# Moving 344 KB of the second dense matrix to the lower half of the partitions, and its products to the early sum

## Chip, cores, metric

One core of one Trainium2 chip. The metric is the device time of one execution in microseconds (us). The kernel before took 192.01 us (median of 4 runs, 191.77 to 192.2).

## What is computed

One decode step for two sequences: a layer norm of `x`, then attention over a window of 4096 cached positions, and beside it a dense layer with the mish activation; the two results and `x` are summed.

```python
xn = _layernorm(x, axis=-1)
return x + _A_ref(xn, k_cache, v_cache, wq, wo) + _B_ref(xn, w1, b1, w2)

# B: D = 448, F = 1792, two rows
h = einsum("bsd,df->bsf", x, w1) + b1
act = h * tanh(softplus(h))
out = einsum("bsf,fd->bsd", act, w2)
```

`w2` is 1792 rows of 448 bf16 numbers, 1.6 MB. The keys, the values and the four weight matrices together are 77.7 MB, and every byte of them is used once.

## The kernel before

**Stages.** The 8 key/value heads and 2 sequences are taken in U = 4 units (`u`), each with four pairs of sequence and head. A unit's keys are two tiles of 4 MB (`load_k`, two halves), its values four tiles of 2 MB (`load_v`, `g` = 0 to 3). Per unit, the vector engine transposes the keys (`turns`, line 267), TensorE makes the scores (`scores`, line 345), ScalarE the exponentials (line 353), and TensorE weighs the values (`values`, line 390). `gather`, `finish` collect the unit's output; `relay` and `mix_early` multiply it by its rows of `wo`.

**Two sums in PSUM.** `early` is a [2, 448] sum of full width: one matmul adds 448 columns. It takes `x` and the units 0 to 2 (`mix_early`, line 472). `carry` copies it to SBUF and from there into `acc`, a sum that is cut into four column groups of 112; `add_rows` (line 247) adds to `acc` with four matmuls, one for each group. The last unit (`mix`) and all of the second dense matrix (`dense_out`) go to `acc`. At the end `acc` is copied to `res` and stored.

**The dense layer.** `w1` is loaded early and used in unit 0 (`dense_in`), then `mish` makes `act_bf`, [128 partitions, 7, 2, 2]. The 1792 inner rows are cut in two halves `k` of 896; partition `p` holds rows 7p to 7p+6 of each half, so `act_bf[p, i, k]` meets row `7p + i` of half `k`. `w2` is loaded in four parts at the very end of the stream, into a buffer of the pool that held the keys: all 7 rows of half 0, then rows 0 to 3, 4 and 5, and 6 of half 1 (`w2_parts`, line 536).

**Order of the transfers.** All large transfers are issued by the SyncE queue (SP) in the order of the program: for each unit u = 0 to 2 the first keys of the next unit, two value tiles, the second keys, two value tiles, the unit's rows of `wo`; then for u = 3 two value tiles, `wo` in two transfers, the third value tile, the fourth in two pieces (24 and 8 of 32 columns), and the four parts of `w2`. An issue waits where its buffer isn't free yet (two buffers for keys and `w2`, three for values) and where its completion semaphore is still held: eight such semaphores are used in turn, so a transfer can't be issued until the eighth transfer before it has landed. `x` and the bias `b1` are issued by ScalarE's queue.

**The last unit on TensorE**, in order: `values(3, 0)`, then `relay(2)`, `mix_early(2)` and `carry()`, then `values(3, 1)`, `values(3, 2)`, `gather`, the fourth value tile (`values_fixed`, line 425), `finish`, `mix`, `dense_out` of the four parts, and the copies to `res`.

Of the kernel before, what the change touches and what calls it, by code (L numbers as in the profile page):

```python
# [11 lines left out]
BF16 = mybir.dt.bfloat16  # L12
FP32 = mybir.dt.float32
# [4 lines left out]
def kernel(  # L18
# [13 lines left out]
    nc = tc.nc  # L32
    P = 128
# [3 lines left out]
    RK = 2  # L37

    Bsz, Sq, D = A_x.shape
# [20 lines left out]
    NI = F2 // P  # L60
# [7 lines left out]
    k_pool = ctx.enter_context(tc.tile_pool(name="kk", bufs=2))  # L68
# [4 lines left out]
    consts = ctx.enter_context(tc.tile_pool(name="consts", bufs=1))  # L73
# [7 lines left out]
    ps_m = ctx.enter_context(tc.tile_pool(name="ps_m", bufs=1, space=PSUM))  # L81

    KE = T * Dh
# [3 lines left out]
    def ring(name):  # L87
        return v_pool.tile([P, KE], BF16, tag="v", name=name)
# [9 lines left out]
    def load_v(u, g, lo=0, hi=T):  # L98
        if lo == 0:
            v_t[u, g] = ring("v")  # L100
        t = v_t[u, g]
        src = vview[u][:, s0:, :].rearrange("j (g x t) d -> g x j (t d)", g=G, x=C)
        nc.sync.dma_start(  # L103
            out=t[:, lo * Dh : hi * Dh], in_=src[g, :, :, lo * Dh : hi * Dh]
        )
# [16 lines left out]
    x_bf = consts.tile([Bsz, D], BF16)  # L122
    nc.scalar.dma_start(out=x_bf[:, :], in_=A_x.flatten_outer_dims())
    b1_sb = consts.tile([P, 2, NI], BF16)
    nc.scalar.dma_start(out=b1_sb[:], in_=B_b1.rearrange("(k q c) -> q k c", k=2, q=P))

    load_k(0, 0)
    wq_t = []
# [7 lines left out]
    ident = consts.tile([P, P], BF16)  # L136
# [9 lines left out]
    for k in range(KU):  # L146
        nc.gpsimd.tensor_copy(
            out=hot[:, k, :, :, k], in_=ident[:].rearrange("p (q y) -> p y q", y=4)
        )
    eps_t = consts.tile([Bsz, 1], FP32)  # L150
    nc.vector.memset(eps_t[:], 1e-5)

# [6 lines left out]
        out=rstd[:], in_=mv[:, 1:2], func=ACT.Sqrt, bias=eps_t[:], scale=1.0  # L159
# [4 lines left out]
        out=xn_bf[:],  # L164
# [8 lines left out]
        out=parm[:], in_=ident[:].rearrange("p (a o) -> p o a", o=2), axis=AXIS.X, op=ALU.add  # L173
# [3 lines left out]
        out=jm[:],  # L177
        in_=ident[:].rearrange("p (a j h) -> p j a h", j=J, h=rep),
# [4 lines left out]
        out=jm[:], in0=jm[:], scalar1=-1.0, scalar2=29952.0, op0=ALU.add, op1=ALU.mult  # L183
# [3 lines left out]
        out=mneg[:], in_=jm[:].unsqueeze(1).to_broadcast([P, TH * 8, J])  # L187
    )
    sel = consts.tile([P, 2, NQ], FP32)
    for x in range(2):  # L190
        for w in range(4):
            at = 32 * w + (2 * (w % 2) + x) * NQ
# [3 lines left out]
            else:  # L196
                nc.vector.tensor_tensor(
                    out=sel[:, x, :], in0=sel[:, x, :], in1=src, op=ALU.add
# [16 lines left out]
    for odd in range(2):  # L215
        for half in range(2):
            o = (half + odd) % 2
            nc.vector.tensor_scalar(
                out=xs[:, odd::2, half * Bsz : (half + 1) * Bsz],
# [6 lines left out]
    early = ps_e.tile([Bsz, D], FP32)  # L226
# [5 lines left out]
    def carry():  # L232
        e_sb = small.tile([P, 2 * Dh], FP32, tag="vs", name="e_sb", bufs=1)[0:Bsz, 0:D]
        nc.scalar.copy(out=e_sb, in_=early[:])
        for g in range(G):
            nc.tensor.matmul(
                acc[32 * g : 32 * g + Bsz, :],
                lhsT=id2[:],
                rhs=e_sb[:, g * DG : (g + 1) * DG],
                start=True,  # L240
                stop=False,
                skip_group_check=True,
            )
# [31 lines left out]
    for n in range(2):  # L275
        for e in range(2):
# [3 lines left out]
                out=sp[:],  # L280
                in_=ident[:, o : o + 63 : 2].unsqueeze(1).to_broadcast([P, G, 32]),
# [81 lines left out]
    state = {}  # L363
# [18 lines left out]
    def values(u, g):  # L382
        if g == 0:
            state["v", u] = ps_v.tile([P, 2, Dh], FP32, tag="v", name="pv")
        pv = state["v", u]
        v = v_t.pop((u, g))
        for k in range(T // 2):
            a, b = k // 2, k % 2
            w = 2 * (a % 2) + b
            nc.tensor.matmul(  # L390
                pv[32 * w : 32 * (w + 1), :, :].rearrange("p x d -> p (x d)"),
                lhsT=p_t[a // 4][:, g, 4 * (a % 4) : 4 * (a % 4) + 4, :].rearrange(
                    "p t q -> p (t q)"
                ),
                rhs=v[:, 2 * k * Dh : (2 * k + 2) * Dh],
                start=(g == 0 and a < 2),
                stop=(g == G - 1 and a >= 6),
                skip_group_check=True,
            )
# [46 lines left out]
    def relay(u):  # L446
        oT = state.pop(("oT", u))
        ox_ps = ps_m.tile([P, 4, 2, Bsz], FP32, tag="m", name="ox_ps")
        for h in range(rep):
            rows = slice(h * 64, (h + 1) * 64)  # L450
            for y in range(4):
                for k in range(KU):
                    nc.tensor.matmul(
                        ox_ps[rows, y, :, :],
                        lhsT=hot[:, k, y, :, :].rearrange("p q k -> p (q k)"),
                        rhs=oT[:, :, k * rep + h, :],
                        start=(y == 0 and k == 0),
                        stop=(y == 3 and k == KU - 1),
                        skip_group_check=True,
                    )  # L460
        ox = small.tile([P, 8, Bsz], BF16, tag="ox", name="ox")
        nc.scalar.copy(  # L462
            out=ox[:].rearrange("p i b -> p (i b)"),
            in_=ox_ps[:].rearrange("p y c b -> p (y c b)"),
        )
        state["ox", u] = ox

    def mix_early(u):
        ox = state.pop(("ox", u))
        w = wo_t.pop(u)[:].rearrange("p k h (c d) -> p (k h c) d", c=2)  # L470
        for i in range(8):
            nc.tensor.matmul(  # L472
                early[:],
                lhsT=ox[:, i, :],
                rhs=w[:, i, :],
                start=False,
                stop=(u == U - 2 and i == 7),
            )
# [8 lines left out]
    act_bf = consts.tile([P, NI, 2, Bsz], BF16)  # L487
# [24 lines left out]
    def mish():  # L512
        h_ps = state.pop("h")
        shape = [P, NI, 2, Bsz]
        h_sb = consts.tile(shape, FP32, name="h_sb")
        nc.vector.tensor_tensor(
            out=h_sb[:],
            in0=h_ps[:],
            in1=b1_sb[:].rearrange("p k i -> p i k").unsqueeze(3).to_broadcast(shape),
            op=ALU.add,  # L520
        )
        u_sb = consts.tile(shape, FP32, name="u_sb")
        nc.scalar.activation(out=u_sb[:], in_=h_sb[:], func=ACT.Exp)
        t_sb = consts.tile(shape, FP32, name="t_sb")
        nc.vector.scalar_tensor_tensor(
            out=t_sb[:], in0=u_sb[:], scalar=2.0, in1=u_sb[:], op0=ALU.add, op1=ALU.mult
        )
        den = consts.tile(shape, FP32, name="den_sb")
        nc.vector.tensor_scalar(
            out=den[:], in0=t_sb[:], scalar1=2.0, scalar2=None, op0=ALU.add  # L530
        )
        nc.vector.reciprocal(out=den[:], in_=den[:])
        nc.vector.tensor_tensor(out=t_sb[:], in0=t_sb[:], in1=den[:], op=ALU.mult)
        nc.vector.tensor_tensor(out=act_bf[:], in0=h_sb[:], in1=t_sb[:], op=ALU.mult)

    w2_parts = ((0, 0, NI), (1, 0, 4), (1, 4, 6), (1, 6, NI))

    def load_w2(part):
        if part == 0:
            state["w2"] = k_pool.tile([P, RK * KE], BF16, tag="k", name="w2")  # L540
        k, lo, hi = w2_parts[part]
        w2_in = B_w2.flatten().rearrange("(k p e) -> k p e", k=2, p=P)
        at = k * NI * D
        nc.sync.dma_start(  # L544
            out=state["w2"][:, at + lo * D : at + hi * D],
            in_=w2_in[k, :, lo * D : hi * D],
        )
# [13 lines left out]
    turns(0, 1)  # L561
    dense_in()
    mish()
    scores(0, 1)
    weigh(0)
    for u in range(U - 1):
# [18 lines left out]
        if u < U - 2:  # L585
            relay(u)
            mix_early(u)
    u = U - 1
    load_v(u, 0)
    load_v(u, 1)  # L590
    load_wo(u)
# [3 lines left out]
    for part in range(len(w2_parts)):  # L595
        load_w2(part)
    for g in range(G - 1):
        values(u, g)
        if g == 0:
            relay(u - 1)  # L600
            mix_early(u - 1)
            carry()
# [48 lines left out]
```

## Time and profile before

| | |
|---|---|
| median of 4 runs | 192.01 us |
| the profiled execution, its own time | 191.54 us |
| its span, first to last instruction | 189.4 us |
| first data packet of the stream | about 2.2 us after the start |
| last landing of an input | 186.44 us |
| moved by DMA | 77.78 MB, 411 GB/s over the span |
| VectorE busy | 89.4 us (47%) |
| TensorE matmuls busy | 85.5 us (45%) |
| ScalarE busy | 12.3 us (7%) |

All times below are counted from the start of the span. A transfer is said to land when the last of its sixteen completion marks (the semaphore events of the trace, one for each DMA engine) has come.

### The profile page before, as it was taken

To read this page: it belongs to the slowest core of one execution; us is meant where nothing else is said; L and a number is where in the kernel's file an instruction comes from. 1 tells how busy PE (TensorE), PEld (TensorE's weight loads), DVE (VectorE), ACT (ScalarE), POOL (GpSimd) and SP (SyncE) were. 2 spreads that over 40 slices of the span, in tenths; PEclk is the share of its full clock that TensorE was granted. 3 is DMA by queue.
4 is the path that set the end of the run, shared out by engine and by line. 5 is a ranking of instruction groups with operands and counts; after the bars stand their busy time and mean duration, and the time that the engine had idled before them with its cause. 6 is when DMAs were issued, how large, how long until landed. Compare 5 with 4: busy or idle time off the path is not lost.

```text
span 189.4 us, 1986 instructions
## 1 busy us (share of the span) xinstructions
PE 85.5 (45%) x870; PEld 37.0 (20%) x873; DVE 89.4 (47%) x81; ACT 12.3 (7%) x23; POOL 3.9 (2%) x16
## 2 busy tenths in 40 slices
PE   0301645455039004878335023867256044956484
PEld 0100121421012001423012011412011011522183
DVE  6619642983990098018940395038910692040001
ACT  3000031001000000110001000110001001011001
POOL 8000000000000000000000000000000000000000
PEclk9999999999999955566858855586756655599555
DMA  6999999999999999999999999999999999999990
GB/s 222 443 384 418 458 422 418 454 439 394 429 491 415 384 420 434 434 436 429 415 460 443 398 412 478 407 415 419 436 450 412 415 424 434 432 398 429 407 382 31
DMA packets 5871, 77.78 MB, mean 411 GB/s; under 512 B 868, under 2 KB 1640, under 8 KB 2408
## 3 DMA queue, kind: packets, MB, share of 16 engines
q1 hardware_dynamic: 5588, 77.66, 96.8%
q8 instruction: 6, 0.10, 0.2%
q10 hardware_dynamic: 276, 0.01, 0.1%
q14 instruction: 1, 0.01, 0.0%
HBM read 77.67 MB, written 0.00 MB: 410 GB/s over the span
## 4 chain that ended last, share of the span: by engine, by line
DMA 82%; PE 8%; DVE 3%; issue 3%; SPq 2%; ACT 1%; DVEq 0%
DMA v<-in_A_v_cache_dram 59%; DMA k<-in_A_k_cache_dram 15%; DMA w<-in_B_w_dram 7%; PE pv L390 4%; DVE kt L267 2%; PE sc L345 2%; PE o L410 1%; DVE p L356 1%; SPq L132 1%; SPq L544 1%; SPq L95 1%; SPq L103 0%; ACT ex L353 0%; PE acc L247 0%; ACT vs L404 0%
## 5 line engine op out<-in xcount | busy, mean ns | idle before, releaser
L267 DVE STREAM_TRANSPOSE kt<-k 128x4096 f32<-128x4096 f32 x16 | 70.1, 4420 | 41.4 <-DMA k<-in_A_k_cache_dram 41.4
L390 PE MATMUL pv<-v,p 128*32 128x512 bf16 x240 | 25.1, 562 | 61.4 <-DMA v<-in_A_v_cache_dram 61.4
L345 PE MATMUL sc<-kt,qd 128*32 128x512 bf16 x256 | 24.8, 554 | 4.6 <-DVE kt L267 2.3
L390 PEld LDWEIGHTS <-p 128*32 128x32 bf16 x240 | 8.2, 120 | 77.2 <-issue 69.3
L437 DVE TENSOR_TENSOR oT<-o,rec 128x16 bf16<-128x16 f32 x4 | 0.7, 174 | 30.9 <-PE o L410 16.6
L356 DVE STREAM_TRANSPOSE p<-ex 128x512 bf16<-128x512 bf16 x8 | 5.2, 690 | 14.6 <-ACT ex L353 14.6
L345 PEld LDWEIGHTS <-qd 128*32 128x32 bf16 x256 | 8.1, 126 | 18.3 <-issue 15.5
L353 ACT ACTIVATE ex<-sc 128x512 bf16<-128x512 f32 x8 | 4.8, 597 | 73.9 <-PE sc L345 73.9
L289 PE MATMUL q_ps<-wq,xs 128*32 128x512 bf16 x28 | 3.4, 625 | 12.1 <-DMA wq<-in_A_wq_dram 12.1
L410 PE MATMUL o<-sel,vs 128*128 128x8 f32 x32 | 7.5, 364 | 2.8 <-ACT vs L404 2.8
L410 PEld LDWEIGHTS o<-sel,vs 128*128 128x128 f32 x32 | 7.1, 326 | 6.4 <-ACT vs L404 6.4
L472 PE MATMUL early<-wo,ox 128*2 128x448 bf16 x24 | 8.0, 499 | 0.8 <-ACT ox L462 0.8
L368 PE MATMUL dn<-p,ones 128*128 128x512 bf16 x8 | 3.5, 434 | 6.4 <-DVE p L356 6.4
L404 ACT COPY vs<-pv 128x512 f32<-128x512 f32 x4 | 2.3, 585 | 54.0 <-PE pv L390 54.0
L502 PE MATMUL h_ps<-xs,w 128*128 128x4 bf16 x49 | 2.8, 193 | 4.3 <-DMA w<-in_B_w_dram 4.3
L210 PE MATMUL xr_ps<-ident,xrows 2*128 2x2 bf16 x7 | 1.0, 181 | 6.6 <-DVE xrows L209 6.6
L376 DVE TENSOR_REDUCE rec<-dn 128x8 f32<-128x512 f32 x4 | 2.8, 692 | 2.1 <-PE dn L368 2.1
L289 PEld LDWEIGHTS <-xs 128*32 128x32 bf16 x28 | 1.0, 126 | 14.0 <-issue 14.0
L502 PEld LDWEIGHTS <-w 128*128 128x128 bf16 x49 | 2.7, 154 | 5.2 <-DMA w<-in_B_w_dram 5.2
L472 PEld LDWEIGHTS <-ox 128*2 128x2 bf16 x24 | 2.3, 105 | 4.6 <-issue 3.0
L334 PE MATMUL sc<-mneg,ident 128*128 128x512 bf16 x5 | 3.0, 591 | 0.0
L368 PEld LDWEIGHTS <-ones 128*128 128x128 bf16 x8 | 0.5, 99 | 8.2 <-DVE p L356 5.9
(62 smaller groups left out, 38.0 us busy)
## 6 DMA issues: line engine op xcount, KB each, us to landing
k<-in_A_k_cache_dram SPq DMA_DIRECT2D x8, 4096.0 KB, 30.3
v<-in_A_v_cache_dram SPq DMA_DIRECT2D x15, 2048.0 KB, 27.3
wo<-in_A_wo_dram SPq DMA_DIRECT2D x3, 896.0 KB, 24.8
wq<-in_A_wq_dram SPq DMA_DIRECT2D x1, 2048.0 KB, 16.9
w<-in_B_w_dram SPq DMA_DIRECT2D x1, 1568.0 KB, 32.2
wq<-in_A_wq_dram SPq DMA_DIRECT2D x1, 1536.0 KB, 19.9
v<-in_A_v_cache_dram SPq DMA_DIRECT2D x1, 1536.0 KB, 11.6
wo<-in_A_wo_dram SPq DMA_DIRECT2D x2, 448.0 KB, 15.5
```

The lines of the kernel that those rows point to most:

```text
L267: nc.vector.transpose(out=kt[i][:, :, :, r, :], in_=t[:, r * KE : (r + 1) * KE].bitcast(FP32).rearrange("p (a c j) -> p a c j", c=P // (R ...
L289: nc.tensor.matmul(q_ps[32 * u : 32 * (u + 1), :], lhsT=xs[:, s, :], rhs=wq_t[s][:, u * 512 : (u + 1) * 512], start=(s == 0), stop=(s == N ...
L334: nc.tensor.matmul(sc[:].rearrange("p t c m -> p (t c m)"), lhsT=ident[:], rhs=mneg[:].rearrange("p a j -> p (a j)"), start=True, stop=Fal ...
L345: nc.tensor.matmul(sc[32 * w : 32 * (w + 1)].rearrange("p t c m -> p t (c m)"), lhsT=qd[:, u, 2 * n + e, :, :].rearrange("p g q -> p (g q) ...
L353: nc.scalar.activation(out=ex[:, :, :, i, :], in_=sc[:], func=ACT.Exp, scale=scale)
L356: nc.vector.transpose(out=p_t[h][:].rearrange("p g t q -> p t g q"), in_=ex[:, h * TH : (h + 1) * TH].rearrange("p t c i m -> p t (c i m)" ...
L368: nc.tensor.matmul(dn[:].rearrange("p a q -> p (a q)"), lhsT=ones[:], rhs=p_t[i][:].rearrange("p g t q -> p (g t q)"), start=(i == 0), sto ...
L376: nc.vector.tensor_reduce(out=rec[:], in_=dn[:].rearrange("p a q -> p q a"), axis=AXIS.X, op=ALU.add)
L390: nc.tensor.matmul(pv[32 * w : 32 * (w + 1), :, :].rearrange("p x d -> p (x d)"), lhsT=p_t[a // 4][:, g, 4 * (a % 4) : 4 * (a % 4) + 4, :] ...
L410: nc.tensor.matmul(po[:, c, :], lhsT=sb[:, x, c::2], rhs=sel[:, x, :], start=(x == 0 and c == 0), stop=(last and x == 1), skip_group_check ...
L472: nc.tensor.matmul(early[:], lhsT=ox[:, i, :], rhs=w[:, i, :], start=False, stop=(u == U - 2 and i == 7),)
L502: nc.tensor.matmul(h_ps[:, i, :, :].rearrange("p k b -> p (k b)"), lhsT=w1_v[:, s, i, :], rhs=xs[:, s, 0 : 2 * Bsz], start=(s == 0), stop= ...
```

## The change

Rows 0 to 2 of the 7 rows that a partition holds of half 1 (128 x 3 x 896 B = 344 KB) no longer come with the other parts of `w2` at the end. They are loaded before the values of the last unit, onto partitions 0 to 63 only: partition 32z + 4a + b takes those of old partition 64h + 32z + 8b + a, for h = 0 and h = 1 one behind the other. Four transfers of 32 partitions with 2688 B each carry them; by the name of the change DMA engines 0 to 7 do. `act_low` holds the activations in the same new order: `mish` makes it with two matmuls against columns of the identity (`perm`) and a copy. Six matmuls of full width (`dense_out_low`, over 64 partitions) add the products to `early`, after `values(3, 0)`. The remaining parts of `w2` are three, and the load of `b1` is cut in five transfers.

```diff
-    nc.scalar.dma_start(out=b1_sb[:], in_=B_b1.rearrange("(k q c) -> q k c", k=2, q=P))
+    b1_in = B_b1.rearrange("(k q c) -> q k c", k=2, q=P)
+    for lo, hi in ((0, 64), (64, 80), (80, 96), (96, 112), (112, P)):
+        nc.scalar.dma_start(out=b1_sb[lo:hi], in_=b1_in[lo:hi])
...
+    perm = consts.tile([P, 4, 8, 4], BF16)
+    nc.gpsimd.tensor_copy(
+        out=perm[:], in_=ident[:].rearrange("p (z b a) -> p z a b", b=4, a=8)
+    )
...
+        ap_ps = ps_m.tile([P, 2, LOW, Bsz], FP32, tag="m", name="ap_ps")
+        for h in range(2):
+            nc.tensor.matmul(
+                ap_ps[0 : P // 2, h, :, :],
+                lhsT=perm[:, 2 * h : 2 * h + 2].rearrange("p z a b -> p (z a b)"),
+                rhs=act_bf[:, 0:LOW, 1, :],
+                start=(h == 0),
+                stop=(h == 1),
+                skip_group_check=True,
+            )
+        nc.vector.tensor_copy(out=act_low[:], in_=ap_ps[0 : P // 2])
-    w2_parts = ((0, 0, NI), (1, 0, 4), (1, 4, 6), (1, 6, NI))
+    LOW = 3
+    act_low = consts.tile([P // 2, 2, LOW, Bsz], BF16)
+    w2_parts = ((0, 0, NI), (1, LOW, 6), (1, 6, NI))
+    low_at = 2 * NI * D
+
+    def load_w2_low():
+        state["w2"] = k_pool.tile([P, RK * KE], BF16, tag="k", name="w2")
+        w2_in = B_w2.flatten().rearrange("(k h z b a e) -> k h z a b e", k=2, h=2, z=2, a=8, b=4)
+        for h in range(2):
+            at = low_at + h * LOW * D
+            for z in range(2):
+                nc.sync.dma_start(
+                    out=state["w2"][32 * z : 32 * (z + 1), at : at + LOW * D],
+                    in_=w2_in[1, h, z, :, :, 0 : LOW * D],
+                )
+
+    def dense_out_low():
+        for h in range(2):
+            for i in range(LOW):
+                at = low_at + (h * LOW + i) * D
+                nc.tensor.matmul(
+                    early[:],
+                    lhsT=act_low[:, h, i, :],
+                    rhs=state["w2"][0 : P // 2, at : at + D],
+                    start=False,
+                    stop=False,
+                )
...
     u = U - 1
+    load_w2_low()
     load_v(u, 0)
...
         if g == 0:
+            dense_out_low()
             relay(u - 1)
             mix_early(u - 1)
             carry()
```

## The prediction

> **What bounds the kernel now.** I read the page's slices first, then the chain of waits, the DMA queues, and the completion marks in the trace.
>
> ```profile
> span 189.4 us, 1986 instructions
> ...
> DMA  6999999999999999999999999999999999999990
> ...
> q1 hardware_dynamic: 5588, 77.66, 96.8%
> q8 instruction: 6, 0.10, 0.2%
> ...
> q14 instruction: 1, 0.01, 0.0%
> ```
>
> The DMA row is the reading: from the second slice to the last but one the sixteen engines have no free time. Nothing on TensorE or VectorE can shorten the run unless the last bytes land earlier. The two lines "instruction" are fetches of program code that use the same engines; inside the span there are six of 16 KB and one of 8 KB. The end of the chain of waits:
>
> ```profile
> 172.06 0.05 issue
> 172.12 14.07 DMA w<-in_B_w_dram
> 186.19 0.04 issue
> 186.23 0.60 PE acc L247 x12
> 186.83 0.24 DVE res L617
> ```
>
> The chain hangs on the last two parts of `w2` (landed 186.19 and 186.44); 12 matmuls, the copies and the store follow. So the question is when the slowest of the sixteen engines ends. The sixteen marks of three transfers, sorted, from the trace's semaphore events:
>
> ```
> w1 (3.25)      35.01 35.03 35.05 35.09 35.11 35.17 35.19 35.22 35.23 35.24 35.25 35.27 35.31 35.33 35.44 35.49
> k, unit 1      64.25 64.26 64.27 64.33 64.34 64.39 64.41 64.43 64.46 64.46 64.47 64.54 64.57 64.70 66.04 66.20
> w2, last part  184.40 184.51 184.52 184.59 184.61 184.61 184.64 184.69 184.73 184.83 185.55 186.06 186.18 186.22 186.38 186.44
> ```
>
> At 35 us all engines are within 0.48 us. After two code fetches (39.84 and 62.80) two are some 1.5 us late. At the end six are late: five by about 1.5 us and one by 0.75 us, ten are not. The packet that shares its engine with a 16 KB fetch shows why: the fetch takes 0.97 to 1.11 us, and the next packet 0.47 to 0.50 us longer than its neighbours (1.71 for 1.21). The lateness is never made up, since no engine is ever idle. The sixth large fetch (183.95) moved no mark; it fell on an engine that had ended.
>
> **What the change does to the marks.** Every engine carries the same bytes before. A part of 3584 B a partition (8 packets an engine) sets the marks 1.06 us later, one of 1792 B 0.56, one of 896 B some 0.25 to 0.30. Between them 8 packets of 2688 B cost 0.81.
> - Taken from every engine at the end: 1.06 + 0.56 - 0.81 = 0.81 us (six rows of half 1 become three).
> - Added to engines 0 to 7: four transfers of 32 x 2688 B on eight engines are 16 packets an engine, 2 x 0.81 plus three marks of 9 ns = 1.65 us.
> - So engines 8 to 15 end 0.81 us earlier, and engines 0 to 7 0.84 us later.
>
> The trace doesn't number the engines. If the six late ones are all in 8 to 15, the late ones end at 186.44 - 0.81 = 185.63 and the latest of the others at 184.83 + 0.84 = 185.67: 0.77 us earlier than now. If a late one is in 0 to 7, it ends at 186.06 to 186.44 + 0.84 = 186.90 to 187.28. These are the two bounds, -0.77 and +0.84, and between them I take the first by the nearest rows: the first packets of the stream start between 2.176 and 2.437, and in that order, followed packet by packet up to each fetch, the engines hit first, third and fifth (39.84, 96.95, 164.95) are tenth, fourteenth and fifteenth of sixteen. If the engines start in the order of their numbers, these three are in 8 to 15. But the one hit by the 8 KB fetch is eighth, and those hit second and fourth belong to a cluster of three that I can't tell apart (second, sixth and twelfth), so that order can hold only in part. The evidence is thin, and so are the chances below.
>
> The Trainium skill has rules on both sides. "DMA: Bandwidth & Descriptors", section "The descriptor swizzle", puts partitions 0 to 63 on engines 0 to 7, which agrees with the name of the change; no row of this trace shows a partition's engine. The same page, "Rules for kernel authors", says of transfers to separate halves of the partitions not to bother, as both spray over all sixteen engines. By that rule each engine would carry 344 KB / 16 in either order, the last mark would stay at 186.44, and the sum would be no gain. What the trace shows is that the number of engines follows the shape: of the sixteen marks of `x` (two rows), only two came with data (2.16 and 2.19).
>
> **The tail.** After the last-but-one landing come three rows of four matmuls where there were two: in the rows at the end (186.23, 186.39, 186.48) a further row costs 0.05 us at most. With the last-but-one landing at 186.19 - 0.81 = 185.38, the last row starts at 185.38 + 0.04 + 0.30 = 185.72, where it started at 186.48. The store's completion semaphore takes another place among eight that SP checks at the end, 0.065 us a check: the worst place costs 0.26, the present one 0; my count of the transfers (47 for 40) puts it one place before the last, +0.07. Sum: -0.76 + 0.07 = -0.69 us.
>
> **Edits that I cost at nothing, and their cover.**
>
> ```profile
> 129.15 8.77 DVE L267 STREAM_TRANSPOSE kt<-k 128x4096 f32<-128x4096 f32 x2 [0.51 <-DMA k<-in_A_k_cache_dram]
> ...
> 135.80 0.60 SPq L110 DMA_DIRECT2D wo<-in_A_wo_dram  x1
> ...
> 140.89 0.54 SPq L103 DMA_DIRECT2D v<-in_A_v_cache_dram  x1
> ...
> 172.81 0.37 PE L236 MATMUL acc<-e_sb,id 2*2 2x112 f32 x8 [0.67 <-ACT e_sb L234]
> 173.11 1.05 PE L390 MATMUL pv<-v,p 128*32 128x512 bf16 x16
> 177.71 1.90 PE L390 MATMUL pv<-v,p 128*32 128x512 bf16 x16 [3.55 <-DMA v<-in_A_v_cache_dram]
> ```
>
> - *Four more issues on SP.* Their buffer is free when the transposes end, 129.15 + 8.77 = 137.92. Four issues of about 0.55 end at 140.1, before the value load at 140.89 that is queued behind them. That load then also waits for the transfer eight before it, now the second keys of unit 3, landed at 148.62: up to 8 us later. Cover: the transfers issued ahead of it keep the engines busy until `wo` lands at 160.59. Without that cover each us late is a us on the run.
> - *Six matmuls into `early`.* `mix_early` takes 1.68 for 8 (0.21 each), in unit 2 3.15 (0.39): 1.3 to 2.4 us. They delay `carry` and `values(3, 1)`, which now ends at 174.16; TensorE then waits 3.55 us for the third value tile. 1.1 us is left at least; past it the fourth tile and `gather` would be late. Twelve `add_rows` matmuls fewer at 185 gain nothing: `w2` is awaited there.
> - *Two matmuls and a copy in `mish`.* `act_bf` is done at 42.24, and `scores(0, 1)`, started at 40.58, now stands behind them on TensorE: about 2 us later, as are the exponentials, the transposes and sums of the weights and, on VectorE, the transposes of unit 1 (47.68 to 49.7). The next keys' issue slips from 56.43 to 58.5 and the value load behind it from 58.47 to 59.1; the queue then holds transfers that land until 78. `values(0, 0)` waits for its tile until 51.60 anyway, and its weights would be ready at 48.8.
> - *Five loads of `b1`* on ScalarE, ahead of the layer norm's root: 4 more issues of 0.42 to 0.53, 2 us, inside the 5.00 us that VectorE idles before its first transposes (13.37). If one of them waits for a semaphore held by the first of the five, which I put at 15 us, the root comes 14 us later, the first transposes end at 31 for 22.14, and the next keys' issue follows; `w1` keeps the engines busy until 34.8. Covered, with 2 us to spare after a latency of 1.4 us.
> - *`perm`* on GpSimd: 0.28 us in a row that ends at 4.6, first needed at 25.4.
>
> **The forecast.** 189.4 - 0.69 = 188.7 of span, 191.54 - 0.69 = 190.85 for this execution. It ran 0.47 below the median, so against the median: 192.01 - 0.69 = 191.32 us, 0.36% faster. Own range 191.0 to 191.7. A difference under 0.2% (0.38 us) can't be told from none.
>
> **Rivals.**
> 1. *A late engine is among 0 to 7.* Place: the last mark of `w2`. Price: 0.46 to 0.84 and 0.07 of tail, 192.5 to 192.9, slower. It decides as soon as one engine of 0 to 7 would have ended after 186.44 - 0.84 = 185.60. For it: two of the places hit, second and fourth, lie in a cluster with members early in the starting order. Against: the three places that are certain lie late in it.
> 2. *The sixth fetch finds its engine busy.* It came at 183.95, just when one of the first engines ended. With 16 more TensorE instructions before it (8 matmuls and their weight loads) it comes some 0.25 us earlier; an engine of 0 to 7 now ends at 185.24 at the earliest, and with 1.5 us more at 186.75, +0.31 and tail: 192.4, at the edge of no change. If it falls on one of 8 to 15 it costs nothing.
> 3. *Only the engine that is 0.75 us late is among 0 to 7*, 185.55 + 0.84 = 186.39; *or the transfers spread over all sixteen*, 186.44. Then the tail alone: 192.0 to 192.1, no change.
>
> **Chances.** Forecast 0.55; rival 1 0.22; rival 2 0.11, half of it slower; rival 3 0.12. Faster 0.55, same 0.12 + 0.05 = 0.17, slower 0.22 + 0.06 = 0.28. The range goes from 190.9 (a tail that costs nothing and a run like the profiled one) to 192.7, the middle of rival 1, which leaves out half of that.
>
> **What would show it.** Right: marks of the last part that lie together, late and early ones within some 0.5 us, the last at 185.6 to 185.7; the value load of unit 3 issued at about 148.6 with no gap in the DMA row; a TensorE wait for the third value tile of 1 to 2.5 us; a code fetch near 183.7 that moves no mark. Wrong: marks at 186.9 or later (rival 1), one single mark 1 us behind the rest (rival 2), the old split of ten and six (rival 3), or a slice of the DMA row under 9.

## The result, and the profile after

| | before | changed |
|---|---|---|
| median | 191.81 us (71 runs, 191.42 to 192.25) | 192.12 us (48 runs, 191.38 to 193.17) |
| ratio, 95% interval | | 1.0014 (1.0008 to 1.002) |
| profiled execution, its span | 191.54, 189.429 us | 191.62, 189.573 us |
| last mark of `w2` | 186.436 | 186.373 |
| start of the last row's matmuls | 186.479 | 186.567 |

The forecast was 0.36% faster. What came is a loss of 0.14%: less than the 0.2% that the prediction calls no difference, but its interval leaves out 1. The span of every run is on record to 0.1 us, and it shows more: its median is 190.1 us over the 48 runs of the changed kernel, and 189.5 to 189.7 in five sets of runs of the kernel before. The profiled execution of the changed kernel (189.573) is among its shortest: three of the 48 are at 189.6 or under. The time outside the span is shorter by some 0.2 us after the change (median 1.94 against 2.09 to 2.17); no trace here shows why. The page after:

```profile
span 189.6 us, 1989 instructions
...
DMA  6999999999999899999999999999999999999990
...
q1 hardware_dynamic: 5604, 77.66, 96.6%
q8 instruction: 6, 0.10, 0.2%
...
q14 instruction: 1, 0.01, 0.0%
```

The engines are as full as before (one slice reads 8), and the same seven fetches of program code ride on them. The end of the chain of waits (start, duration, engine, tile and line) has changed:

```profile
160.95 17.45 DMA v<-in_A_v_cache_dram
178.41 0.04 issue
178.45 1.92 PE pv L396 x16
...
180.45 0.59 ACT vs L410
181.04 0.04 issue
181.09 1.88 PE o L416 x8
182.96 1.71 PE o L431 x64
184.68 0.02 issue
184.70 0.18 DVE oT L443
184.89 0.04 issue
184.93 1.98 PE acc L253 x40
186.91 0.25 DVE res L660
```

In this execution it no longer hangs on `w2`. It hangs on the third value tile of unit 3, which landed at 178.41 (before: 177.67). Behind it come the last unit's steps on TensorE, ScalarE and VectorE, with no wait for another transfer. The marks say why the tile was late, and why the last mark hardly moved (sorted; of the low transfers the eight that come with data):

```
low transfers, the first  159.02 159.05 159.08 159.15 159.16 159.22 159.23 | 160.08
w2, last part             183.78 184.03 184.09 | 185.29 185.31 185.33 185.34 185.40 185.46 185.47 185.48 185.50 185.51 185.52 185.55 | 186.37
```

Of the engines 0 to 7 seven are on time and one is 0.85 us late; none is 1.5 us late. At the end twelve engines are level (seven on time with 1.65 us more to carry, five late ones with 0.81 less), three are early, and the single half-late engine of 0 to 7 sets the last mark: 185.55 + 0.84 = 186.39 was the sum of rival 3, 186.37 came.

### The profile page after: what moved, and what is told of

The parts are those of the page before. It is cut to its first block, busy times and chain, and to the rows that moved or that the text cites. A ratio compares the mean times of both kernels' runs of the same rounds, so it can differ in the third digit from the quotient of the medians.

```text
span 189.6 us, 1989 instructions
## 1 busy us (share of the span) xinstructions
PE 93.2 (49%) x866; PEld 38.6 (20%) x869; DVE 89.2 (47%) x82; ACT 12.3 (6%) x23; POOL 4.2 (2%) x17
## 4 chain that ended last, share of the span: by engine, by line
DMA 85%; PE 7%; DVE 3%; issue 3%; SPq 1%; ACT 0%; DVEq 0%; ACTq 0%
DMA v<-in_A_v_cache_dram 56%; DMA k<-in_A_k_cache_dram 16%; DMA wo<-in_A_wo_dram 13%; PE pv L396 4%; DVE kt L273 2%; PE acc L253 1%; PE o L416 1%; PE o L431 1%; ACT vs L410 0%; SPq L103 0%; SPq L116 0%; SPq L95 0%; DVEq L689 0%; DVE res L660 0%; DVE h_sb L522 0%
## 5 line engine op out<-in xcount | busy, mean ns | idle before, releaser
L396 PE MATMUL pv<-v,p 128*32 128x512 bf16 x240 | 27.6, 610 | 52.1 <-DMA v<-in_A_v_cache_dram 52.1
L351 PE MATMUL sc<-kt,qd 128*32 128x512 bf16 x256 | 27.8, 607 | 2.8 <-issue 1.4
L396 PEld LDWEIGHTS <-p 128*32 128x32 bf16 x240 | 8.7, 127 | 69.8 <-issue 64.7
L374 PE MATMUL dn<-p,ones 128*128 128x512 bf16 x8 | 4.3, 541 | 6.0 <-DVE p L362 6.0
L216 PEld LDWEIGHTS <-xrows 2*128 2x128 bf16 x7 | 0.7, 99 | 9.2 <-DVE xrows L215 8.9
```

What stands on the lines that cost most here:

```text
L351: nc.tensor.matmul(sc[32 * w : 32 * (w + 1)].rearrange("p t c m -> p t (c m)"), lhsT=qd[:, u, 2 * n + e, :, :].rearrange("p g q -> p (g q) ...
L374: nc.tensor.matmul(dn[:].rearrange("p a q -> p (a q)"), lhsT=ones[:], rhs=p_t[i][:].rearrange("p g t q -> p (g t q)"), start=(i == 0), sto ...
L396: nc.tensor.matmul(pv[32 * w : 32 * (w + 1), :, :].rearrange("p x d -> p (x d)"), lhsT=p_t[a // 4][:, g, 4 * (a % 4) : 4 * (a % 4) + 4, :] ...
```

## The experiments

Three ends of the run lie close together, and the experiments sort them: the **marks** of the engines, the **TensorE chain** behind the third value tile, and the **program**. The last was not in my prediction; the first runs brought it up. In the kernel before, TensorE's last 11 matmuls start 2.33 to 2.57 us after the sixth 16 KB fetch does (five profiles), which I read as the time until the block of code with them is there.

**Where the late engines are.** Probes of n rows of 128 B in the kernel before, queued behind `wo` of unit 3: n marks with data come, from n engines.

```diff
+    for n in (2, 4, 6, 7):
+        probe = consts.tile([16, 64], BF16, name=f"probe{n}")
+        nc.sync.dma_start(out=probe[0:n, :], in_=B_w2[0:n, 0:64])
```

> The kernel before with four small extra loads (2, 4, 6 and 7 rows of 128 B) between the last unit's wo and its third value tile; a transfer of n rows ends in n marks with data, from n engines. Theory (the 8 KB program fetch made one engine of 0 to 7 late by 0.75 us, the 16 KB fetches five of 8 to 15): the marks of these probes lie within 0.5 us but for one that is 0.75 us behind; from which probe on it is there tells its number: in none means engine 7. Rival A (the eight-engine transfers of the change themselves make one engine late): no late mark in any probe. Rival B (a 16 KB fetch hit one of 0 to 6): a mark 1.5 us behind.

The second kernel has n = 9, 10, 12, 14.

> The same with probes of 9, 10, 12 and 14 rows. Theory: each has one mark 0.75 us behind (the engine of 0 to 7), and marks 1.5 us behind that grow with the number of rows, to between two and five at 14 rows, none of them among the first eight. Rival B: as many at 9 rows as at 14.

```
 4 rows  171.28 171.32 171.42 172.11
 7 rows  170.98 171.17 171.31 171.65 171.68 171.77 172.48
10 rows  171.11 171.12 171.18 171.18 171.20 171.20 171.33 171.39 171.44 | 172.14
12 rows  171.31 171.33 171.35 171.38 171.38 171.38 171.52 171.58 171.65 | 172.33 | 172.62 172.67
14 rows  171.50 171.53 171.54 171.56 171.57 171.58 171.69 171.76 171.86 | 172.51 | 172.65 172.68 172.79 172.85
```

With two rows both marks were on time, with four one was 0.7 us late: the half-late engine is 2 or 3. With 10 rows none is 1.5 us late beside it, 12 rows add two, 14 two more: engines 10 to 13 are late and the fifth is 14 or 15, if the engines are taken in the order of their numbers. So the five that matter do lie in 8 to 15, and the sixth does not. The low marks of the changed kernel say the same without that condition: of the engines that carry them none is 1.5 us late and one is half-late. And since the probes find it in the kernel before, the low transfers did not make it late.

**Fewer rows in the low transfers**, `LOW = 1` and `LOW = 2` for 3:

> The changed kernel with one row of seven moved instead of three (115 KB). Theory: each row moved takes 0.27 us from every engine at the end and adds 0.28 to engines 0 to 7, so the five late engines of 8 to 15 end at 186.44 - 0.27 = 186.17 and the half-late one of 0 to 7 at 185.55 + 0.28 = 185.83; the third value tile lands no later than before. Marks 0.27 us earlier, tail 0.07 longer: ratio 0.999. Rival A (the moved bytes cost what they save): ratio 1.000 to 1.001. Rival C (TensorE's chain from the third value tile sets the end in the changed kernel, the marks don't matter): 1.000.

> Two rows moved (229 KB). Theory: late engines at 186.44 - 0.54 = 185.90, the half-late one at 185.55 + 0.56 = 186.11: last mark 0.33 us earlier; the third value tile lands 0.16 us later than before, TensorE still waits for the marks: ratio 0.9986. Rival A: 1.000 to 1.001, between one row and three. Rival C: about 1.0005.

Measured 1.0006 (0.9998 to 1.0015) and 0.9999 (0.9987 to 1.0011): both expectations missed. With one row the last mark came at 185.98, earlier still than the 186.17 expected, and the run ended later than before. Chain of waits, `LOW = 1`:

```profile
185.75 0.53 PE acc L253 x13
186.29 0.56 issue
186.84 0.45 PE acc L253 x9
```

TensorE stood 0.56 us with all data landed ("issue": no wait that the profile shows). Its sixth fetch started at 184.48, the last 11 matmuls at 186.84, 2.36 us later. That is what the program as an end of its own would look like, and the next runs test it. With two rows the one profile has its last mark at 186.22 (186.11 expected) and no such pause, but its span of 189.3 does not stand for the rest: eight of the twelve runs have 189.8 to 190.1.

**Taking the program wait away by leaving work out.**

```diff
-        if u < U - 2:
+        if 0 < u < U - 2:
             relay(u)
             mix_early(u)
```

> The kernel with one row moved, and unit 0's relay and mix_early left out (its part is missing from the output): 48 TensorE instructions fewer, so that none is left for the last block of program. Theory (with one row moved TensorE's last matmuls waited for the sixth program fetch, 2.36 us after its start): no idle of TensorE without a releaser at the end, the last row starts 0.04 us after the last mark (about 186.0): 0.4 us less, ratio 0.998. Rival C (TensorE's chain from the third value tile, or anything else but the program, held the end): same as with the part, 1.0005.

> The kernel before, with unit 0's relay and mix_early left out. Theory: the last mark (186.44) still sets the end, the program's wait (until 186.38 before) is gone with nothing behind it: ratio 0.9990 to 1.0000. If the program alone set the end before: 0.998 or less.

> The changed kernel without unit 0's relay and its early mix (that part of the output is left out): fewer TensorE instructions, so the last block of the program is fetched earlier, as in the two runs of this kind before. If the arrival of that block sets the changed kernel's end as it does the one before: 0.997 to 0.9985 of the kernel before, 0.3 to 0.4% under the change. If the marks of the engines 0 to 7, later by 0.84 us, have taken its place: 1.000 to 1.0015, as the change itself (1.0014).

Measured: `LOW = 1` 0.9974 (0.9964 to 0.9984), before 0.9973 (0.9964 to 0.9982), changed kernel 1.0004 (0.9995 to 1.0013). The ratio of the first is as expected and the pause before the last 11 matmuls is gone, but its profile has the last mark at 186.40, where about 186.0 was expected, and the last row at 186.58. The second is better than the 0.999 to 1.000 that I had put, and lies where I had put "the program alone". The third lies in the range of its second case (the marks have taken the program's place), but it tells little, because the cut moved the fetches: the third of them came at 101.4 in place of 96.7, and the low transfers now had three late marks of eight (161.58, 161.85, 162.05 beside 160.23 to 160.66), with the last mark at 187.09.

**Other splits.** Ten engines (transfers of 40 partitions, two rows), and the change with its single load of `b1` back:

```diff
-    LOW = 3
+    LOW = 2
+    LOW_N = (40, 40, 40, 8)
...
```

> Two rows of seven moved, on engines 0 to 9 (three transfers of 40 partitions on ten engines, one of the last 8 partitions on eight), products in eight matmuls of full width; b1 in six pieces, so that the store's check is the last of SP's five. Theory (engines 10 to 14 are late by 1.5 us, one of 2 and 3 by 0.75 us; each row moved takes 0.27 us from all and adds 0.17 net to engines 0 to 9): late engines at 186.44 - 0.54 = 185.90, the half-late one at 185.55 + 0.34 = 185.89, the third value tile as early as before, and the sixth program fetch 0.5 us earlier, with its engine's end. Last row of matmuls 0.5 us earlier: ratio 0.9972. Rival A (the moved bytes cost what they save): 1.000.

```diff
-    for lo, hi in ((0, 64), (64, 80), (80, 96), (96, 112), (112, P)):
-        nc.scalar.dma_start(out=b1_sb[lo:hi], in_=b1_in[lo:hi])
+    nc.scalar.dma_start(out=b1_sb[:], in_=B_b1.rearrange("(k q c) -> q k c", k=2, q=P))
```

> The changed kernel with b1 in one load again. The five pieces are not on the path of the stream; with four transfers fewer the store's completion semaphore is checked first of SP's five, with four checks of 0.065 us behind it instead of one: 0.2 us longer than the change, ratio to before 1.0024. Rival: the five pieces cost time at the start; then 1.0005 or less.

Ten engines: 1.0033 (1.0022 to 1.0043), a clear miss. Three of the ten were late (the first of the transfers has marks at 159.90, 160.58 and 161.15 beside 159.04 to 159.42), the last mark came at 187.28. The single `b1`: 1.0022 (1.0009 to 1.0035) for 1.0024 expected. The store's check did come first of five, with four of 0.065 us behind it. But in that profile two engines of 0 to 7 were late and the last mark was at 186.69, so this ratio does not show the checks alone. The profile does: from the start of the first copy to the end of the span it takes 2.85 us, in the changed kernel 2.67.

**The changed kernel three times more**, letter for letter:

> The changed kernel once more, letter for letter, for one more profiled execution. Theory (where the six late engines lie changes from execution to execution, or from build to build): of three such looks at least two differ from one another in how many of the eight marks of the low transfers are late at 159 to 161 us, and in the last mark: none or one half-late among engines 0 to 7 gives a last mark of 185.6 to 186.4 and a span of 189.3 to 189.7; one that is 1.5 us late among them gives 186.7 to 187.4 and a span of 189.9 to 190.6. Rival (the places are fixed with the kernel): always one mark of eight late, by 0.85, and the last at 186.4 within 0.1.

> As for the first look: by the theory another split of the late marks in at least one of the three, with the last mark and the span following it; by the rival the same one mark of eight, 0.85 late, and the last mark at 186.4 within 0.1.

> As for the first look: by the theory another split of the late marks in at least one of the three, with the last mark and the span following it; by the rival the same one mark of eight, 0.85 late, and the last mark at 186.4 within 0.1.

In all three one of the eight low marks was half-late, as in the first profile. The theory that the places of the first five fetches change from execution to execution fell: four executions had the same split. Its rival missed too: a last mark of 186.4 came in none of the three. What changed is the sixth fetch:

| execution of the changed kernel | run | span | sixth fetch | last mark | last row starts |
|---|---|---|---|---|---|
| first | 191.62 | 189.573 | 183.48 | 186.37 | 186.57 |
| second | 192.12 | 190.342 | 184.74 | 187.15 | 187.35 |
| third | 191.83 | 190.048 | 184.60 | 186.80 | 187.05 |
| fourth | 191.74 | 189.956 | 184.47 | 186.87 | 186.94 |

In the first profile the fetch moved no mark: the three early engines were ending just then, and one of their mark packets ended at 183.481, with the fetch's start. In the other three it came later and moved a mark. Third execution, last part: eleven marks from 185.23 to 185.63, the half-late one at 186.43, and a new one at 186.80, which is one of the twelve level engines 1.2 to 1.6 us late. In the second execution the chain hangs on `w2` itself once more, and in the third there is a pause:

```profile
173.23 13.72 DMA w<-in_B_w_dram
186.94 0.04 issue
186.98 0.71 PE acc L253 x16
```

```profile
184.95 1.84 PE acc L253 x69
186.79 0.25 issue
187.03 0.36 PE acc L253 x7
```

There TensorE goes on at 187.03, again 2.4 us after the fetch's start. This is rival 2, a mark moved, and the late block besides. With spans of 190.0 to 190.3 these three are the common case: 44 of the 48 runs have 189.8 or more.

**The kernel before twice more:**

> The kernel before once more, letter for letter. Theory (the last program block ends it as often as the marks do): where the sixth 16 KB fetch starts later than 184.1 us, TensorE stands idle before its last 11 matmuls until that start plus 2.4 us, the last row starts later than 186.5 and the span is over 189.5; the last mark stays at 186.3 to 186.6 whatever the fetch does, since all engines carry the same bytes and a seventh late one is no later than the five. Rival (no such wait in the kernel before): fetch at 183.9 to 184.0 and a span of 189.4 in each look.

> As for the first look at the kernel before: by the theory the span follows the sixth fetch's start plus 2.4 us and not the last mark, which stays at 186.3 to 186.6.

Sixth fetch at 183.91 and 183.87, last marks 186.42 and 186.34, spans 189.53 and 189.37. Neither case was met cleanly. The fetch is steady (183.87 to 184.04 in five executions of the kernel before, the two with probes among them), and in the three without probes the program arrives within 0.1 us of the last mark; with the second set of probes it came 0.22 us after it (186.44 for 186.22). In the first of the two executions here it is the later one, by a hair:

```profile
186.21 0.25 PE acc L247
186.48 0.45 PE acc L247 x11
```

**Taking the program wait away with the full output kept:** one set of relay matmuls for units 0 and 1.

```diff
-        if u < U - 2:
-            relay(u)
-            mix_early(u)
+        if u == 1:
+            relay((0, 1))
+            mix_early(0)
+            mix_early(1)
...
-                        rhs=oT[:, :, k * rep + h, :],
+                        rhs=oT[:, :, :, k * rep + h, :],
```

> The kernel before with the relays of units 0 and 1 as one set of matmuls over both (16 matmuls and their 16 weight loads fewer, nothing of the output left out). 1743 matmul and weight-load records become 1711; the last block of the program, which held the last 22 before, is then not needed. If that block's arrival set the end of the kernel before: 0.9965 to 0.9985 of its time. If the gain of the run without unit 0's relay came from the work left out: 0.9995 to 1.0005.

> The changed kernel with the same merged relays: no wait for the last program block either. Against the kernel before: if that wait alone made the change slower, as much as the merged kernel before within 0.0007 (0.9965 to 0.9985). If it is the engines 0 to 7 (0.84 us more each, whether late by earlier fetches or hit by the sixth): last mark 186.4 to 187.3, 0.9985 to 1.0015, and 0.1 to 0.4% over the merged kernel before.

Before, merged: 191.29 against 191.66 us, 0.998 (0.9971 to 0.9989). This version beats both kernels. Its sixth fetch came at 184.61 and nothing waited for it; the last row follows the last mark (186.432) by 0.04. The pause is gone: the eight products of the third part of `w2` start between 186.229 and 186.286, where in the kernel before the second came 0.15 us after the first. The spans gain as the times do: a median of 189.2 us over the 11 runs, 189.5 for the kernel before beside them.

Changed, merged: 1.0011 (1.0002 to 1.002), 0.31% over the merged kernel before. So the program wait alone isn't what makes the change slow; the case "engines 0 to 7" held. It is no clean subtraction, since the merge moved the fetches too (the third to 101.28 from 96.69). In its profile three engines of 0 to 7 are late (161.47, 161.77, 161.88 beside 160.19 to 160.62), and the end is the TensorE chain:

```profile
160.78 18.18 DMA v<-in_A_v_cache_dram
179.00 1.92 PE pv L396 x14
...
185.48 1.98 PE acc L253 x76
187.46 0.25 DVE res L671
```

The third value tile landed at 178.96, the last row began 8.15 us later at 187.11, 0.19 after the last mark (186.92).

**Chain or marks.** The merged change with the low transfers behind that tile in the queue:

```diff
-    load_w2_low()
     load_v(u, 0)
     load_v(u, 1)
     load_wo(u)
     load_v(u, 2)
+    load_w2_low()
...
-            dense_out_low()
```

> The changed kernel with merged relays, and the four low transfers behind the third value tile of unit 3 in the queue instead of ahead of the first two; the six products on them are left out, as their rows come too late for the early sum. The last marks stay as in the merged change (the same bytes on the same engines), the third tile comes 0.8 to 1.6 us earlier. If the chain of TensorE work behind that tile set the end of the merged change (1.0011): 0.998 to 0.9995, with the last row right behind the last mark. If the marks of the engines 0 to 7 set it: 1.0005 to 1.0015.

The tile landed at 177.56, 1.4 us earlier, and the last row (186.849) followed the last mark (186.807) by 0.04: the chain was gone from the end. The ratio is 1.0005 (0.9997 to 1.0014), the lower edge of the case "marks", and its interval overlaps that of the merged change. So the chain shows 0.15 us in the profile and 0.06% in the ratio; which of it and the marks weighs more stays open.

**One row, with merged relays:**

> The change with one row of half 1 instead of three in the low transfers (engines 0 to 7 later by 0.28 us at the end, 8 to 15 earlier by 0.27), with merged relays and the full output. Engines late in 0 to 7 now cost at most 0.3 us on either end: 0.997 to 0.999 of the kernel before, beside 0.998 for the merged kernel before; over 1.0 would mean that the low transfers cost something besides the bytes they put on engines 0 to 7.

0.998 (0.9971 to 0.999), as expected, and the same as the merged kernel before. The pause of `LOW = 1` is gone:

```profile
173.08 13.03 DMA w<-in_B_w_dram
186.16 0.77 PE acc L253 x24
```

But the equal times hide a difference. The median span is 189.6 us over its 11 runs, as in the kernel before, while the merged kernel before has 189.2; what it gains in time lies outside the span (1.84 us for 2.09). Inside the span one row on engines 0 to 7 gains nothing.

## Why the prediction was wrong

**The step that failed** is "between them I take the first": that all six late engines are in 8 to 15. Five were, and the half-late one was not. That is rival 3, to which I gave 0.12. In the first profile it takes the forecast away by itself: last mark 186.37 for the 185.67 forecast. The evidence for the step was the starting order of the packets, and I had noted that the place of just that engine spoke against it (eighth of sixteen, as were two in a cluster that I couldn't resolve). The arithmetic was right, the choice between the bounds was not one that the trace could carry.

**A second term, put at nothing, failed as well:** the sixth fetch, which "moved no mark" in the kernel before and has no part in the sum. In three of four profiled executions of the changed kernel it moved the last mark to 186.80 to 187.15, past where the half-late engine ended (186.43 to 186.51). By these marks it would have taken the gain away even with the half-late engine in 8 to 15.

**Two ends that the prediction did not have.**
- The TensorE chain. I had 3.55 us of wait ahead of the third value tile and took them as cover for six matmuls. They were: 1.41 us for the six, and 1.45 us of wait left. But the low transfers also stand ahead of that tile on engines 0 to 7, so the tile itself is late by 0.74 us. From its landing to the last row TensorE needs 8.15 us in the changed kernel. The kernel before has three rows of `w2` more on this stretch, 0.09 us each where nothing is awaited: 177.67 + 8.15 + 0.27 = 186.1, 0.4 us ahead of the row that the marks released (186.48). The change used this slack up and 0.09 us more, which is where its last row started (186.57). The 0.05 us a row in the prediction's tail was read behind a pause, where rows start closer together. The timeline of the changed kernel, with the six products and what is left of the wait:

```profile
171.14 1.41 PE L573 MATMUL early<-w,act_low 64*2 64x448 bf16 x6
...
178.45 1.90 PE L396 MATMUL pv<-v,p 128*32 128x512 bf16 x16 [1.45 <-DMA v<-in_A_v_cache_dram]
```

- The program. I read the sixth fetch as harmless, since it moved no mark in the kernel before. What hangs on its bytes I didn't ask. The pause of 0.15 us between two matmuls of the last rows (186.230 and 186.378) was in the trace, and I took the rows to wait for their data alone.

**Rival 2** (0.11, priced 192.4) is what three of four profiled executions of the changed kernel show, with spans 0.5 to 0.9 us over 189.43. It came about otherwise than forecast: the fetch was not 0.25 us earlier than 183.95 but 0.5 to 0.8 us later. Together with rival 3 it accounts for the sign: the half-late engine is enough to undo the forecast's 0.77 us, and the sixth fetch makes most executions longer than before. Only the first profile, the fifth fastest of the 48 runs, shows rival 3 without it. That the median came so near rival 3's price (192.0 to 192.1) is partly luck: the span is half a microsecond longer, and the time outside it shorter.

**Rival 1**, a 1.5 us late engine in 0 to 7, did not happen in the changed kernel. Its like came in four relatives with other code (the cut one, the merged one, the single `b1` and the ten engines): more than one late mark among the low transfers, and last marks of 186.69 to 187.28. With one row, the cut and the merged kernel have three and two late marks of eight.

**Rules.** The Trainium skill's page "DMA: Bandwidth & Descriptors" ("Rules for kernel authors") says that halves of the partitions spray over all sixteen engines anyway. The four transfers here do otherwise: each has 32 partitions from a source whose outermost size is 8, eight marks come with data, and their lateness stays with the same engines. No run moves half of the partitions in one transfer. The section "The descriptor swizzle", which the prediction cites for partitions 0 to 63, lists one transfer of 128 partitions. "Runtime: NRT & Kernel Launch" ("Instruction fetch mechanics") says that code comes in blocks of 16 KiB and that its fetch is hidden by the prefetch. The blocks agree (16384 B a packet), the hiding doesn't: 0.56 us of idle TensorE with one row in the low transfers, gone in both kernels with fewer instructions.

**What held.** The net sums: the half-late engine went from 185.55 to 186.37, 0.82 for 0.84, and the five late ones from 186.06 to 186.44 into the group of 185.29 to 185.55, for 0.81 less. The tail: the store's check stands one place before the last, and the span grew by 0.144 where the last copy began 0.09 later. The covers: `scores(0, 1)` 2.4 us later (42.94), the next keys' issue at 57.95 (58.5 forecast), the value load of unit 3 at 148.54 (148.6 forecast), `b1` and `perm` without a trace in the first transposes (13.24). These lines show the issues:

```profile
129.06 8.72 DVE L273 STREAM_TRANSPOSE kt<-k 128x4096 f32<-128x4096 f32 x2
...
136.43 0.60 SPq L110 DMA_DIRECT2D wo<-in_A_wo_dram  x1
137.81 3.03 SPq L564 DMA_DIRECT2D w<-in_B_w_dram  x4
...
148.54 0.58 SPq L103 DMA_DIRECT2D v<-in_A_v_cache_dram  x1
```

**Open.** Why the sixth fetch of the same kernel starts at 183.48 once and at 184.47 to 184.74 three times, with TensorE at the same place within 0.2 us, no run settles. The profiled execution of the merged kernel before (span 189.38) is no shorter than those of the kernel before (189.37 to 189.53), though the median of the spans is. Taking the program wait away goes with a gain in time in four pairs (the kernel before and `LOW = 1`, each cut and merged), but only for `LOW = 1` does a profile show a wait of that size, and there some 0.2 us of the gain lie outside the span.

## What to carry to other kernels

When every engine is full to the end, ask for each of the last arrivals what else ends within a microsecond of it: here the marks, the work behind an earlier tile, and the code itself lay within 0.4 us, and moving one only handed the end to the next. A load balanced against the lateness of single engines is balanced against something that moves with the code; the same three rows met one, two or three late engines when other instructions changed, 48 at the most. Instructions are bytes as well: 16 matmuls fewer made the kernel before 0.2% faster, and 344 KB put elsewhere made it no faster.

## What the runs showed of the hardware

- A 16 KB code fetch takes 0.97 to 1.11 us on one data engine in the seven profiles of the two kernels (0.88 to 1.36 with other code) and leaves it some 1.5 us late. By the probes, and if transfers of few rows take the engines in the order of their numbers, the late ones were 10, 11, 12, 13 and one of 14 and 15; the 8 KB fetch hit engine 2 or 3. The low marks showed the same split in four executions of one kernel, and other splits with other code.
- TensorE went on 2.33 to 2.60 us after the start of the last fetch that it waited for, of which the fetch's packet takes 0.97 to 1.02.
- The sixth fetch began within 5 ns of the end of a mark packet in 16 of 20 profiles (within 60 ns in three, 169 ns in one); of the 100 earlier fetches of 16 KB one did. Mark packets lie close together there (27 or 28 from 183.4 to 184.8 in three profiles), so chance alone would give about one in five. The trace doesn't say on which engine the packet was; that the fetch waits for the end of a transfer on its own engine is a guess.
